# Turning the decayed keys for the state update on VectorE and through HBM instead of on TensorE, in a fused RWKV-6 and SiLU kernel

## The chip, the cores and the metric

The kernel runs on one core of a Trainium2 chip. The metric is the device time in microseconds of one execution. The profile is one execution of the same program, with 646.2 us from its first to its last instruction.

The engines are called by the names of the profile: PE is TensorE (PEld its weight loads), DVE is VectorE, ACT is ScalarE, POOL is GpSimd, SP is SyncE, which here issues transfers. An engine name with a q (SPq, ACTq) is the queue's own instructions, among them the issue of a transfer.

## The reference

Two blocks follow each other: a linear attention with a decay per channel, and a feed-forward block with SiLU.

```python
B, H, S, D = 4, 8, 768, 48
for t in range(S):
    kt, vt, rt, wt = k[:, :, t], v[:, :, t], r[:, :, t], w[:, :, t]
    cur = einsum('bhd,bhe->bhde', u * kt, vt)
    y[:, :, t] = einsum('bhd,bhde->bhe', rt, state + cur)
    state = wt[..., None] * state + einsum('bhd,bhe->bhde', kt, vt)
x = y.transpose(0, 2, 1, 3).reshape(3072, 384)     # tokens by model width
h = x @ w_in                                       # 384 by 2048
out = (h / (1 + exp(-h))) @ w_out                  # 2048 by 384
```

The change touches the last line of the loop only: the sum over the tokens of key times value that is added to the state.

## The kernel before

**Units.** The sequence is cut into 6 chunks of 128 tokens, and the 4 batches into 2 pairs. A unit is one chunk of one pair, so there are 12 units, numbered 0 to 11. A unit has 2 batches (index b) of 8 heads. Two heads are stacked on the partitions (64 rows each, of which 48 are channels), so that a batch has 4 tiles of 128 partitions by 128 tokens, numbered p; e is the head within the tile.

**Attention in a unit.** The recurrence inside a chunk is solved in 7 levels with doubling block sizes. `tk` holds the keys, channels on the partitions and tokens along the free dimension, in 16 rows of 128 tokens: 8 rows of "own" keys (batch and p), and two rooms of 4 rows each, X[0] and X[1], in which the odd blocks of a level are put together for the score matmuls. At each level POOL multiplies keys by decays (`grow_keys`, L491), DVE does so with the queries `tr`, and PE makes scores (`score_products`, L527). After level 6 the own keys hold, for each token, the key with the decay up to the end of the chunk. The second batch is kept with its tokens in reverse order.

**Then the unit's end.** `y_state` (L652) multiplies the old state by the queries, `y` (L665) adds score times value, ACT copies the sum to `yt` (L669), and `move_x` (L715) sends it by 10 transfers into `xt`, the input of the feed-forward block. `update` (L679) contracts keys and values over the tokens into `p_kv`; POOL decays the old state (L684), and DVE adds the two (L693). For this contraction the tokens have to lie on the partitions. In the units 2 to 11 `turn_k` does that: 4 transposes on PE for each batch (L639), 8 in a unit, and one copy on ACT from PSUM to `kq` for each batch (L640). In the last two units `update` returns at once, since no chunk follows; `turn_k` is run there all the same.

**The feed-forward block** of earlier units fills PE beside this. `up` (L757, 12 instructions of PE, 8 calls in a unit) writes `p_h`, which has two buffers and is emptied by SiLU on ACT (L763). `quarter` (L820, 7 calls in a unit) is a block product of the second weight by a scheme with 7 products instead of 8; its operands are made by `sums` on DVE (L802), and its result leaves through DVE (L829) and ACT (L827).

**What sets the order.** The program is written with a schedule by hand: each engine runs its instructions in the order in which they were emitted and stops at one whose wait is not met. Units 0 to 2 are written out step by step. For the units 3 to 11 `mix(i)` gives groups of steps of the attention, and after each group `ROOM` says how many steps of the feed-forward block follow. Before the change `turn_k` is a group of its own, with two calls of `up` ahead of it and one behind, then come `y_state`, `y`, `update` and `move_x`.

**Transfers.** Nearly all are issued by SP, in the order of emission. `load_blocks` (L106) fetches w, k and r of the unit after next in pieces of 32 tokens, 48 transfers in a unit. `load_values` (L119, L126), `load_rk` (L90) and the 4 small `diag` transfers (L425) are on the same queue, as are the results (L833). [...]

Of the kernel before, what the change touches and what calls it, by code (L numbers as in the profile page):

```python
# [8 lines left out]
F32 = mybir.dt.float32  # L9
# [29 lines left out]
def kernel(  # L39
# [11 lines left out]
    nc = tc.nc  # L51

    B, H, S, D = r.shape
    DM, DF = moe_w_in.shape
    L = 128
    NL = 7
    NB = 2
    NP = H // 2
    PD = 64
    Q = NB * NP  # L60
    NX = Q + 2 * NP
    X = 0, NP + Q
# [4 lines left out]
    NSLOT = 2  # L67
    NTOK = 2
# [28 lines left out]
    def load_blocks(i, name, g):  # L97


        n, b0 = units[i]  # L100
        src, t0 = {"w": w, "r": r, "k": k}[name], n * L + g * 32
        room = raw[:, i % NSLOT, WRK[name]].rearrange("p b h d -> p (b h d)").rearrange("p (q g d) -> p q g d", q=Q, d=32)
        for e in range(2):
            for a in range(2):
                d0, d1 = a * 32, min(D, a * 32 + 32)
                nc.sync.dma_start(out=room[(2 * e + a) * 32:(2 * e + a + 1) * 32, :, g, 0:d1 - d0],  # L106
                                  in_=src[b0:b0 + NB, e::2, t0:t0 + 32, d0:d1].rearrange("b q t d -> t (b q) d"))

    def load_values(i):
# [18 lines left out]
    def load_rk(i):  # L128

        for x, src in enumerate((r, k)):  # L130
            load_twos(tokens_rk[:, x].rearrange("p h s d -> p h (s d)"), src, i, [nc.sync] * NB)


    rounding = ExitStack()
    p_w = rounding.enter_context(tc.tile_pool(name="pr", bufs=1, space=bass.MemoryType.PSUM)).tile([128, 2, 512], F32, name="p_w")
# [188 lines left out]
    def turn(i, b, name):  # L324
        dst = {"w": tw, "r": tr, "k": tk}[name]
        if i not in dst:
            rows = NX if name == "k" else Q
            t = pt.tile([128, rows, L], F32, name="t" + name, bufs=2 if name == "r" else 1)
            dst[i] = [t] if name == "w" else t
        t = dst[i][0] if name == "w" else dst[i]  # L330
        if i < NTOK:
            if (i, b, name) not in turned:
                turn_in(i, b, name)
            turn_out(i, b, name, t)
        else:
            row0 = b * NP + (NP if name == "k" else 0)
# [17 lines left out]
    def turn_out(i, s, name, t):  # L354
        p_tr = turned.pop((i, s, name))
        if name == "k":
            to = t[:, NP:].rearrange("p q (i s) -> p q i s", s=2)
# [96 lines left out]
    def keys(i, start, *dims):  # L454
        k = tk[i][:]
        return bass.AP(tensor=k.tensor, offset=k.offset + start, ap=[k.ap[0], *dims])

    def odd_keys(i, l):

        c, blocks = 1 << l, NP * (L >> (l + 2))  # L460
        nc.scalar.copy(out=keys(i, X[(l + 1) % 2] * L + c, [4 * c, blocks], [c, 2], [1, c]),  # L461
                       in_=keys(i, NP * L + c, [4 * c, blocks], [NP * L + c, 2], [1, c]))

    def odd_products(i, l, b, *dims, skip=0):

# [10 lines left out]
    def grow_keys(i, l):  # L476
        c, ni = 1 << l, L >> (l + 1)
        x_at, next_at = X[l % 2], X[(l + 1) % 2]
        for b in range(NB):
            row0 = NP + b * NP  # L480
            if l + 1 < NL:
                start = [next_at * L, row0 * L][b] + b * c
                step = 2 * c + (1 - 2 * b) * (row0 - next_at) * L
                out = keys(i, start, [4 * c, NP * ni // 2], [step, 2], [1, c])
                have = keys(i, x_at * L + b * c, [4 * c, NP * ni // 2], [2 * c, 2], [1, c])
                blocks = [[4, NP * ni // 2], [2, 2]]
            else:
                out = keys(i, row0 * L + b * c, [L, NP], [1, c])
                have = keys(i, x_at * L + b * c, [L, NP], [1, c])
                blocks = [[2, NP]]  # L490
            nc.gpsimd.tensor_tensor(out=out, in0=have, in1=odd_products(i, l, b, *blocks), op=ALU.mult)  # L491
        if i < NTOK:
            product(i, l)

    def odd_ones(i):

        nc.scalar.copy(out=keys(i, X[1] * L + 1, [1, NB], [4, NP * L // 4], [1, 1]),
                       in_=keys(i, NP * L + 1, [NP * L + 1, NB], [4, NP * L // 4], [1, 1]))

    def start_keys(i, engine, own):  # L500

        n = NP * L // 4
        for b in range(NB):
            x = b if own else 1 - b
            at = (NP + b * NP) * L + b
# [116 lines left out]
    def turn_apart(i):  # L622

        apart[i] = [ps.tile([128, NB, NP, D], F32, name="p_sc", bufs=2) for e in range(2)]
        for x in range(Q):
            for e, to in enumerate(apart[i]):
                rows = slice(PD * e, PD * e + D)
                nc.tensor.transpose(to[:, x // NP, x % NP], tk[i][rows, NP + (x if x < NP else NP + Q - 1 - x), :],
                                    ident[rows, rows])

    def turn_k(i, b):
        kq[i, b] = pt.tile([128, NP, 2 * PD], F32, name="kq")
        if i < NTOK:
            for e, have in enumerate(apart[i]):
                nc.scalar.copy(out=kq[i, b][:, :, PD * e:PD * e + D], in_=have[:, b])
            return
        p_tr = ps.tile([128, NP, 2 * PD], F32, name="p_m", bufs=2)
        for p in range(NP):
            nc.tensor.transpose(p_tr[:, p, :], tk[i][:, NP + (p, 2 * NP - 1 - p)[b], :], ident)  # L639
        nc.scalar.copy(out=kq[i, b], in_=p_tr)  # L640

    p_yt, p_kv, yt = {}, {}, {}

# [27 lines left out]
    def update(i, b):  # L671
        n, b0 = units[i]
        if n == S // L - 1:
            return
        if b == 0:
            p_kv[i] = ps.tile([128, NB, NP, D], F32, name="p_m" if i < NTOK else "p_sc", bufs=2)
        for p in range(NP):
            for e in range(2):
                nc.tensor.matmul(p_kv[i][PD * e:PD * e + D, b, p, :], lhsT=kq[i, b][:, p, PD * e:PD * e + D],  # L679
                                 rhs=values(i, b)[:, 2 * p + e, :], start=(b == 0 and p == 0),  # L680
                                 stop=(b == NB - 1 and p == NP - 1))
        new = state[:, b0 + b]
        if n > 0:
            nc.gpsimd.tensor_tensor(out=new, in0=new,  # L684
                                    in1=tw[i][NL][:, b * NP:(b + 1) * NP, :].to_broadcast([128, NP, 2 * PD]),
                                    op=ALU.mult)
        if b < NB - 1:
            return
        for e in range(2):
            rows, cols = slice(PD * e, PD * e + D), slice(PD * e, PD * e + D)  # L690
            new = state[rows, b0:b0 + NB, :, cols]
            if n > 0:
                nc.vector.tensor_tensor(out=new, in0=p_kv[i][rows], in1=new, op=ALU.add)  # L693
            else:
                (nc.scalar.copy if i == 0 else nc.vector.tensor_copy)(out=new, in_=p_kv[i][rows])
# [23 lines left out]
    def both(fn, i, *args):  # L719
        return [(fn, i, b, *args) for b in range(NB)]  # L720
# [4 lines left out]
    def mix(i):  # L725
# [6 lines left out]
                  [(burst, i, 3), (keep_level, i, 3), (bonus_sum, i, 0), (bonus, i, 1), (bonus, i, 2)],  # L732
                  [(keep_level, i, 4), (go_on, i, 4)],
                  [(prepare, i, 5), (bonus_sum, i, 1)] + ([(load_rk, i + 1)] if i + 1 < len(units) else []),
                  [(burst, i, 5), (keep_level, i, 5)], [(keep_level, i, 6), (go_on, i, 6), (bonus_spread, i), (bonus_write, i)],
                  both(turn_k, i), [*both(y_state, i), *both(y, i), *both(update, i), (move_x, i)]]

        loads = block_loads(i + NSLOT) if i + NSLOT < len(units) else []
        if i + 1 < len(units):
# [164 lines left out]
    for m in range(6):  # L904
# [7 lines left out]
    do(blocks[2], (burst, 2, 3), (keep_level, 2, 3), (keep_level, 2, 4), (go_on, 2, 4), (prepare, 2, 5), (bonus, 2, 1),  # L912
       (bonus, 2, 2), (down, 0, 1, 2), (bonus_sum, 2, 1), (load_rk, 3), (sums, 1, 1), *blocks[3:7], (down, 0, 1, 3))
    do((burst, 2, 5), (keep_level, 2, 5), (keep_level, 2, 6), (go_on, 2, 6), (up, 1, 6), (bonus_spread, 2), (bonus_write, 2),
       (load_values, 3), *both(turn_k, 2), (weight_sums, 2), (up, 1, 7), (sums, 1, 2))
    do((sums, 1, 3), *both(y_state, 2), *both(y, 2), *both(update, 2), (move_x, 2),
       *blocks[7:])

    ROOM = 1, 1, 0, 2, 1, 1, 1, 1, 1, 2, 1, 2, 1, 0
    for i in range(3, len(units)):  # L920
        steps = downs(i - 2) + ups(i - 1)
        groups = mix(i)
# [40 lines left out]
```

## Time and profile before

| | us |
|---|---|
| time, median of 3 runs | 647.81 (647.59 to 648.37) |
| span of the profiled execution | 646.2 |
| PE busy, of the span | 639.6 (99%) |
| DVE busy | 433.9 (67%) |
| POOL busy | 283.1 (44%) |
| ACT busy | 203.8 (32%) |
| the 80 transposes of L639, sum of PE's busy time | 10.4 |
| the 20 copies of L640, sum of ACT's busy time | 10.7 |

Share of busy time alone doesn't say what bounds a kernel, so the profile also follows the chain of work that ended last, back from the last instruction: at each step to what released it. A row of that chain has the start, the length and the instructions it merges. A row of a group of instructions has the line, engine and operation, the tiles and shapes, the count, then the busy time, the mean in ns of one, and the idle time ahead of it with what ended that. A row of transfers has the count, the size and the median time from the issue to the landing. The transposes of this kernel have a pattern on PE that repeats from the third unit on with a period of 50.94 us (324.61 to 375.55 us for L639 in the chain).

### The profile page before, as it was taken

How to read it: one execution, taken by the hardware profiler on the slowest of the kernel's cores; microseconds unless marked ns; L12 is line 12 of the kernel's file. 1: busy time of each engine (PE TensorE's matmuls, PEld its weight loads, DVE VectorE, ACT ScalarE, POOL GpSimd, SP SyncE). 2: the span in 40 equal slices, each digit the busy share in tenths (PEclk: the TensorE clock that was granted, in tenths of full speed). 3: DMA queues.
4: the chain of work that ended last, by engine and by line, in shares of the span. 5: the costliest groups of instructions: out<-in, count | busy, mean ns of one | idle time of the engine just before them, and what ended most of it. 6: DMA issues, size and time to landing. Idle time of an engine off the chain costs nothing.

```text
span 646.2 us, 12889 instructions
## 1 busy us (share of the span) xinstructions
PE 639.6 (99%) x4878; PEld 579.2 (90%) x4878; DVE 433.9 (67%) x737; ACT 203.8 (32%) x408; POOL 283.1 (44%) x356
## 2 busy tenths in 40 slices
PE   8999999999999999999999999999999999999998
PEld 7888876898899899899899899899899989989997
DVE  7879789896777677586586586676586766751031
ACT  5798872212321321320321231231232232131120
POOL 6898398466065054254334425416416505510000
PEclk9999999999999999999999999999999999999999
DMA  9975954433534524513513513423432022000000
GB/s 229 276 180 131 229 129 50 91 75 52 96 63 69 96 49 72 88 31 64 98 29 67 96 28 58 96 37 52 90 54 38 26 50 50 27 2 25 25 0 25
DMA packets 201134, 49.21 MB, mean 76 GB/s; under 512 B 188912, under 2 KB 195952, under 8 KB 201072
## 3 DMA queue, kind: packets, MB, share of 16 engines
q1 hardware_dynamic: 199488, 47.79, 36.5%
q10 hardware_dynamic: 1584, 0.59, 0.4%
q8 instruction: 39, 0.64, 0.4%
q14 instruction: 23, 0.19, 0.1%
HBM read 39.52 MB, written 4.72 MB: 68 GB/s over the span
## 4 chain that ended last, share of the span: by engine, by line
PE 95%; DVE 2%; POOL 1%; ACT 1%; issue 1%; POOLq 0%; DVEq 0%; ACTq 0%
PE p_h L757 39%; PE p_o L820 31%; PE p_sc L527 6%; PE p_m L527 4%; PE p_m L776 3%; PE p_m L665 3%; PE p_m L652 3%; PE p_m L639 1%; PE p_sc L679 1%; POOL tk L491 1%; PE p_m L350 1%; PE p_m L855 1%; PE p_m L703 0%; DVE score L450 0%; POOL w_in_sb L227 0%
## 5 line engine op out<-in xcount | busy, mean ns | idle before, releaser
L757 PE MATMUL p_h<-xt,w_in_sb 128*128 128x256 f32 x1152 | 258.4, 382 | 0.7 <-POOL tk L507 0.7
L757 PEld LDWEIGHTS p_h<-xt,w_in_sb 128*128 128x128 f32 x1152 | 215.8, 190 | 32.5 <-POOL tk L507 0.9
L763 ACT ACTIVATE gt<-p_h 128x512 f32<-128x512 f32 x93 | 55.5, 596 | 228.2 <-PE p_h L757 228.1
L491 POOL TENSOR_TENSOR tk<-tk,tw 128x256 f32<-128x256 f32 x144 | 102.1, 732 | 23.3 <-ACT tk L461 16.6
L537 DVE COPY_PREDICATED score<-mask,p_sc 128x512 f32<-128x512 int8 x78 | 64.1, 885 | 59.7 <-PE p_sc L527 59.4
L820 PE MATMUL p_o<-own,temps 128*128 128x192 f32 x528 | 90.3, 328 | 0.4 <-DVE temps L829 0.4
L820 PE MATMUL p_o<-w_out_sb,gt 128*128 128x192 f32 x528 | 90.4, 328 | 0.0
L820 PEld LDWEIGHTS p_o<-own,temps 128*128 128x128 f32 x528 | 85.8, 190 | 1.8 <-DVE temps L829 0.7
L820 PEld LDWEIGHTS p_o<-w_out_sb,gt 128*128 128x128 f32 x528 | 85.9, 190 | 0.9 <-issue 0.4
L684 POOL TENSOR_TENSOR state<-state,tw 128x512 f32<-128x512 f32 x16 | 19.3, 1225 | 118.5 <-PE p_m L652 118.5
L386 POOL TENSOR_TENSOR tw<-tw 128x256 f32<-128x256 f32 (+6 forms) x83 | 39.8, 480 | 54.5 <-DVE tw L338 50.6
L802 DVE TENSOR_TENSOR temps<-gt 128x256 f32<-128x256 f32 x88 | 44.3, 504 | 21.9 <-ACT gt L763 21.9
L461 ACT COPY tk<-tk 128x256 f32<-128x256 f32 x60 | 24.6, 410 | 83.4 <-PE p_sc L527 40.8
L527 PEld LDWEIGHTS p_sc<-tr,tk 48*128 48x128 f32 x640 | 39.2, 186 | 12.1 <-issue 8.9
L473 DVE TENSOR_TENSOR tr<-tr,tw 128x512 f32<-128x512 f32 x53 | 46.0, 868 | 3.3 <-POOL tk L491 1.0
L527 PE MATMUL p_sc<-tr,tk 48*128 48x128 f32 x640 | 47.1, 285 | 0.6 <-POOL tk L491 0.6
L408 POOL TENSOR_TENSOR ruk<-tokens_rk 128x768 f32<-128x768 f32 x10 | 18.6, 1858 | 65.8 <-DVE own_sums L415 65.8
L595 DVE TENSOR_TENSOR tr<-tr,tw 128x512 f32<-128x512 f32 x29 | 39.9, 1375 | 1.3
L537 DVE COPY_PREDICATED score<-mask,p_m 128x512 f32<-128x512 int8 x54 | 35.4, 706 | 0.0
L820 PE MATMUL p_o<-w_out_sb,temps 128*128 128x192 f32 x176 | 30.4, 326 | 0.0
L829 DVE TENSOR_TENSOR partial<-p_o,partial 128x192 f32<-128x192 f32 x33 | 11.6, 353 | 27.6 <-PE p_o L820 27.6
L597 ACT COPY tr<-tr 128x512 f32<-128x512 f32 x29 | 18.4, 634 | 35.8 <-DVE tr L473 35.0
(144 smaller groups left out, 753.3 us busy)
## 6 DMA issues: line engine op xcount, KB each, us to landing
w_out_sb<-in_moe_w_in_dram SPq DMA_DIRECT2D x6, 768.0 KB, 6.9
tokens_rk<-in_r_dram SPq DMA_DIRECT2D x20, 192.0 KB, 3.4
tokens_rk<-in_k_dram SPq DMA_DIRECT2D x20, 192.0 KB, 3.8
w_out_sb<-in_moe_w_out_dram SPq DMA_DIRECT2D x4, 768.0 KB, 6.3
own<-in_moe_w_out_dram SPq DMA_DIRECT2D x4, 768.0 KB, 5.8
xt<-yt SPq DMA_DIRECT2D x60, 48.0 KB, 2.0
raw<-in_w_dram SPq DMA_DIRECT2D x80, 32.0 KB, 2.2
raw<-in_k_dram SPq DMA_DIRECT2D x80, 32.0 KB, 2.4
```

Source lines behind the costliest of these rows:

```text
L386: engine.tensor_tensor(out=up, in0=t[:, :, 0::2], in1=t[:, :, 1::2], op=ALU.mult)
L461: nc.scalar.copy(out=keys(i, X[(l + 1) % 2] * L + c, [4 * c, blocks], [c, 2], [1, c]), in_=keys(i, NP * L + c, [4 * c, blocks], [NP * L + ...
L473: nc.vector.tensor_tensor(out=odd, in0=odd, in1=tw[i][l][:, :, 0::2][:, :, :, None].to_broadcast([128, Q, L >> (l + 1), c]), op=ALU.mult)
L491: nc.gpsimd.tensor_tensor(out=out, in0=have, in1=odd_products(i, l, b, *blocks), op=ALU.mult)
L527: nc.tensor.matmul(bass.AP(tensor=s_p.tensor, offset=s_p.offset, ap=[s_p.ap[0], [apart * L // 2, 2], [1, L // 2]]), lhsT=tk[i][rows, X[l % ...
L537: nc.vector.copy_predicated(out=dst, mask=masks[l][:, :, None].to_broadcast([128, NB, NP, ni, c]), data=sc[e].rearrange("p (b q) (i c) -> ...
L595: nc.vector.tensor_tensor(out=new[:, :, :, 1, :], in0=old[:, :, :, 1, :], in1=tw[i][l][:, :, 0::2][:, :, :, None].to_broadcast([128, Q, L ...
L652: nc.tensor.matmul(p_yt[i, b][:, p, :], lhsT=state[:, b0 + b, p, :], rhs=tr[i][:, b * NP + p, :], start=(p == 0), stop=False)
L757: nc.tensor.matmul(p_h[:, a, :], lhsT=w_in_sb[:, c, f * 128:(f + 1) * 128], rhs=xt[i][:, c, :], start=(c == 0), stop=(c == KC - 1))
L763: nc.scalar.activation(out=gt[i, m], in_=p_h, func=AF.Silu)
L802: nc.vector.tensor_tensor(out=out, in0=one, in1=two, op=op)
L820: nc.tensor.matmul(p, lhsT=left(f), rhs=right[:, f, :], start=(f == 0), stop=(f == FH - 1))
```

## The change

From unit 2 on the keys are turned without PE. VectorE transposes each block of 32 by 32 in two instructions, from the own rows of `tk` into its first 8 rows, which are no longer needed after the last scores. A block then has its tokens and channels exchanged, but the blocks stand in the wrong places: the partition still says which 32 channels, and the free dimension which 32 tokens. Four transfers write the blocks to a scratch tensor in HBM in runs of 128 bytes, and four transfers read them back in runs of 512 bytes, so that they land at the right place in `kq`. The units 10 and 11 turn no keys at all. To make room for the transposed blocks, X[1] moves ahead of the own keys (rows 0 to 3, 4 to 7, and 8 to 15). `kq` is now one buffer for both batches. From unit 5's data on, the r part of `load_blocks` is issued by ACT instead of SP. The purpose is to free PE, PSUM and ACT from the turning.

```diff
-    X = 0, NP + Q
+    X = 0, NP
+    OWN = 2 * NP
...
-                nc.sync.dma_start(out=room[...], in_=src[...])
+                queue = nc.scalar if i > NTOK + NSLOT and name == "r" else nc.sync
+                queue.dma_start(out=room[...], in_=src[...])
...
+    scratch = ctx.enter_context(tc.tile_pool(name="scratch", bufs=2, space=bass.MemoryType.DRAM))
...
     def turn_k(i, b):
-        kq[i, b] = pt.tile([128, NP, 2 * PD], F32, name="kq")
-        if i < NTOK:
-            for e, have in enumerate(apart[i]):
-                nc.scalar.copy(out=kq[i, b][:, :, PD * e:PD * e + D], in_=have[:, b])
-            return
-        p_tr = ps.tile([128, NP, 2 * PD], F32, name="p_m", bufs=2)
-        for p in range(NP):
-            nc.tensor.transpose(p_tr[:, p, :], tk[i][:, NP + (p, 2 * NP - 1 - p)[b], :], ident)
-        nc.scalar.copy(out=kq[i, b], in_=p_tr)
+        if b == 0:
+            kq[i] = pt.tile([128, NB, NP, 2 * PD], F32, name="kq", bufs=1)
+        for e, have in enumerate(apart[i]):
+            nc.scalar.copy(out=kq[i][:, b, :, PD * e:PD * e + D], in_=have[:, b])
+
+    def turn_blocks(i):
+        for b in range(NB):
+            nc.vector.transpose(out=tk[i][:, b * NP:(b + 1) * NP, :], in_=tk[i][:, OWN + b * NP:OWN + (b + 1) * NP, :])
+        kept = scratch.tile([32, Q, 4, 4, 32], F32, name="kept_keys")
+        for x in range(4):
+            nc.sync.dma_start(out=kept[:, :, :, x].rearrange("t q g d -> t (q g) d"),
+                              in_=tk[i][x * 32:(x + 1) * 32, 0:Q].rearrange("t q (g d) -> t (q g) d", d=32))
+        kq[i] = pt.tile([128, NB, NP, 2 * PD], F32, name="kq", bufs=1)
+        for g in range(4):
+            nc.sync.dma_start(out=kq[i][g * 32:(g + 1) * 32].rearrange("t b q d -> t (b q) d"),
+                              in_=kept[:, :, g].rearrange("t q x d -> t q (x d)"))
...
+        back = b == 1 and i >= NTOK
-                nc.tensor.matmul(p_kv[i][...], lhsT=kq[i, b][:, p, PD * e:PD * e + D],
+                nc.tensor.matmul(p_kv[i][...], lhsT=kq[i][:, b, NP - 1 - p if back else p, PD * e:PD * e + D],
...
-                  [(burst, i, 5), (keep_level, i, 5)], [(keep_level, i, 6), (go_on, i, 6), (bonus_spread, i), (bonus_write, i)],
-                  both(turn_k, i), [*both(y_state, i), *both(y, i), *both(update, i), (move_x, i)]]
+                  [(burst, i, 5), (keep_level, i, 5)],
+                  [(keep_level, i, 6), (go_on, i, 6), (bonus_spread, i), *[(turn_blocks, i)] * (i < len(units) - NB), (bonus_write, i)],
+                  [*both(y_state, i), *both(y, i), *both(update, i), (move_x, i)]]
...
-       (load_values, 3), *both(turn_k, 2), (weight_sums, 2), (up, 1, 7), (sums, 1, 2))
+       (load_values, 3), (turn_blocks, 2), (weight_sums, 2), (up, 1, 7), (sums, 1, 2))
...
-    ROOM = 1, 1, 0, 2, 1, 1, 1, 1, 1, 2, 1, 2, 1, 0
+    ROOM = 1, 1, 0, 2, 1, 1, 1, 1, 1, 2, 1, 3, 0
```

`ROOM` loses the entry of the removed group and keeps its sum: three calls of `up` now stand between the turning and `y_state`.

More of the change, by code (lines that the diff above doesn't have):

```diff
@@ L105, in load_blocks @@
                 d0, d1 = a * 32, min(D, a * 32 + 32)
-                nc.sync.dma_start(out=room[(2 * e + a) * 32:(2 * e + a + 1) * 32, :, g, 0:d1 - d0],
+                queue = nc.scalar if i > NTOK + NSLOT and name == "r" else nc.sync
+                queue.dma_start(out=room[(2 * e + a) * 32:(2 * e + a + 1) * 32, :, g, 0:d1 - d0],
                                   in_=src[b0:b0 + NB, e::2, t0:t0 + 32, d0:d1].rearrange("b q t d -> t (b q) d"))
@@ L335, in turn @@
         else:
-            row0 = b * NP + (NP if name == "k" else 0)
+            row0 = b * NP + (OWN if name == "k" else 0)
             to, back = t[:, row0:row0 + NP, :], name == "k" and b == 1
@@ L356, in turn_out @@
         if name == "k":
-            to = t[:, NP:].rearrange("p q (i s) -> p q i s", s=2)
+            to = t[:, OWN:].rearrange("p q (i s) -> p q i s", s=2)
             nc.scalar.copy(out=to[:, 0:NP, :, s], in_=p_tr[:, :, 0])
@@ L461, in odd_keys @@
         nc.scalar.copy(out=keys(i, X[(l + 1) % 2] * L + c, [4 * c, blocks], [c, 2], [1, c]),
-                       in_=keys(i, NP * L + c, [4 * c, blocks], [NP * L + c, 2], [1, c]))
+                       in_=keys(i, OWN * L + c, [4 * c, blocks], [NP * L + c, 2], [1, c]))
     def odd_products(i, l, b, *dims, skip=0):
@@ L479, in grow_keys @@
         for b in range(NB):
-            row0 = NP + b * NP
+            row0 = OWN + b * NP
             if l + 1 < NL:
@@ L497, in odd_ones @@
         nc.scalar.copy(out=keys(i, X[1] * L + 1, [1, NB], [4, NP * L // 4], [1, 1]),
-                       in_=keys(i, NP * L + 1, [NP * L + 1, NB], [4, NP * L // 4], [1, 1]))
+                       in_=keys(i, OWN * L + 1, [NP * L + 1, NB], [4, NP * L // 4], [1, 1]))
     def start_keys(i, engine, own):
@@ L504, in start_keys @@
             x = b if own else 1 - b
-            at = (NP + b * NP) * L + b
+            at = (OWN + b * NP) * L + b
             have = keys(i, at + 2 * x, [4, n], [1, 1])
@@ L627, in turn_apart @@
                 rows = slice(PD * e, PD * e + D)
-                nc.tensor.transpose(to[:, x // NP, x % NP], tk[i][rows, NP + (x if x < NP else NP + Q - 1 - x), :],
+                nc.tensor.transpose(to[:, x // NP, x % NP], tk[i][rows, OWN + (x if x < NP else NP + Q - 1 - x), :],
                                     ident[rows, rows])
     def turn_k(i, b):
-        kq[i, b] = pt.tile([128, NP, 2 * PD], F32, name="kq")
-        if i < NTOK:
-            for e, have in enumerate(apart[i]):
-                nc.scalar.copy(out=kq[i, b][:, :, PD * e:PD * e + D], in_=have[:, b])
-            return
-        p_tr = ps.tile([128, NP, 2 * PD], F32, name="p_m", bufs=2)
-        for p in range(NP):
-            nc.tensor.transpose(p_tr[:, p, :], tk[i][:, NP + (p, 2 * NP - 1 - p)[b], :], ident)
-        nc.scalar.copy(out=kq[i, b], in_=p_tr)
+        if b == 0:
[13 more added lines that the diff above has]
+                              in_=kept[:, :, g].rearrange("t q x d -> t q (x d)"))
     p_yt, p_kv, yt = {}, {}, {}
@@ L676, in update @@
             p_kv[i] = ps.tile([128, NB, NP, D], F32, name="p_m" if i < NTOK else "p_sc", bufs=2)
+        back = b == 1 and i >= NTOK
         for p in range(NP):
             for e in range(2):
-                nc.tensor.matmul(p_kv[i][PD * e:PD * e + D, b, p, :], lhsT=kq[i, b][:, p, PD * e:PD * e + D],
+                nc.tensor.matmul(p_kv[i][PD * e:PD * e + D, b, p, :], lhsT=kq[i][:, b, NP - 1 - p if back else p, PD * e:PD * e + D],
                                  rhs=values(i, b)[:, 2 * p + e, :], start=(b == 0 and p == 0),
```

## The prediction

> **What bounds the kernel now.** I read the busy shares first, then the chain that ended last, then a unit of that chain in order of time.
>
> ```profile
> PE 639.6 (99%) x4878; PEld 579.2 (90%) x4878; DVE 433.9 (67%) x737; ACT 203.8 (32%) x408; POOL 283.1 (44%) x356
> PE 95%; DVE 2%; POOL 1%; ACT 1%; issue 1%; POOLq 0%; DVEq 0%; ACTq 0%
> ```
>
> PE is both the busiest engine and 95% of the chain. So what leaves PE is a gain, and whatever makes PE wait is a loss at full price. The chain from 324 us on shows the end of a middle unit (start, length, work):
>
> ```profile
> 324.61 0.87 PE p_m L639 x8
> 325.48 2.59 PE p_h L757 x12
> 328.07 1.78 PE p_m L652 x16
> 329.86 1.88 PE p_m L665 x32
> 331.74 0.72 PE p_sc L679 x32
> 332.46 10.60 PE p_o L820 x64
> ```
>
> The eight key transposes take 0.87 us of the chain. Between them and their reader, `update` (L679), lie 2.59 + 1.78 + 1.88 = 6.25 us of other work on PE. PE runs in order: if the keys aren't there when `update` is next, nothing behind it runs, though the quarters (L820) don't need them. The timeline of the same stretch gives ACT and SP:
>
> ```profile
> 321.25 2.50 DVE L450 COPY_PREDICATED score<-own_mask,both_b 128x1024 f32<-128x1024 int8 x2
> ...
> 331.79 0.58 ACT L669 COPY yt<-p_m 128x512 f32<-128x512 f32 x1 [0.29 <-PE p_m L665]
> ```
>
> The second copy to `yt` ends at 332.37, that is 0.63 us after PE's last `y` matmul (331.74). Unit 2 is different. There SP is the busy one:
>
> ```profile
> 122.57 2.10 SPq L106 DMA_DIRECT2D raw<-in_w_dram  x4
> 124.71 6.85 SPq L106 DMA_DIRECT2D raw<-in_k_dram  x12
> 131.66 0.40 SPq L782 DMA_DIRECT2D out_dram<-ob  x1
> 132.15 0.39 SPq L119 DMA_DIRECT2D vt<-in_v_dram  x1
> 132.64 2.15 SPq L126 DMA_DIRECT2D vq<-in_v_dram  x4
> 134.90 5.29 SPq L715 DMA_DIRECT2D xt<-yt  x8
> ```
>
> It issues one transfer after the other up to 134.8 us, while unit 2's `update` runs at 127.34 (chain of waits).
>
> [...]the trace has this instruction at 0.67 us for 128x512 (L338). [...]
>
> ```profile
> L855 PE MATMUL p_m<-ident x16: 421/421/476, 1.4 to 4.6; 128*128 128x128 f32 x16
> ```
>
> The same instruction takes 273 ns at 11.7 us; the first sixteen filled 3.68 us, sixteen later ones 1.97.
>
> **The change part by part.**
>
> *Removed from PE:* 8 transposes in each of the units 2 to 11, 10 x 0.87 = 8.7 us of the chain. This is the most that can be won. The 20 ACT copies of 0.59 us (L640) go too; ACT is 32% busy, so they give nothing.
>
> *Added on VectorE:* 2 x 0.67 = 1.3 us a unit ahead of the bonus write (L450), which ends at 323.75 before and about 325.1 then; `y` needs it at 329. Hidden. What VectorE does behind (the sums, instructions of 0.42 us) ends late by about that, but the wait below leaves room. The moved X[1] and the new row index cost nothing: same instructions, same shapes.
>
> *The trip through HBM, units 5 to 9.* The transposes end at about 322.6. If the eight transfers then ran freely, they would arrive near 332. But the waits in the changed kernel's instructions tell another story. [...] In the units 5 to 9 the fourth write to the scratch waits for the second of the 8 r loads that ACT issues at the unit's end. In ACT's order these stand behind the two copies to `yt`, and those wait for `y` on PE. So the last write can't go out before PE has finished `y`, exactly when PE wants the keys. From the end of `y`:
>
> - copy to `yt` ends: 0.63
> - second r load goes out one issue later (0.45, the median of L106): 1.08
> - it lands 2.2 later (median of the raw loads): 3.3
> - the fourth write goes out and lands. No row has 128-byte runs to HBM. Nearest are 1.9 us (results, 192 KB) and 3.8 (`tokens_rk`, 192 KB in 384-byte runs); I take the 2.9 of `vt`, 1024 runs of 192 bytes, as many runs as here: 6.2
> - the four reads wait for all writes; the last goes out three issues of 0.6 later (L715): 8.0
> - it lands 2.6 later (`vq`; bounds 2.0 from `xt` and 3.8): 10.6
>
> PE waits 10.6 us, by the bounds 8.0 to 13.2 (issues up to 0.65, raw landing 2.4). Queued behind `update` on PE are the quarters; behind the state's addition (L693) on VectorE the next unit's transposes (L338), and POOL waits for these. So the whole pattern shifts. Afterwards PE runs cold: like the start of the trace, about 1.7 us lost (bounds 0 and 2.5[...]); I take 1.8. Net: 10.6 + 1.8 - 0.87 = 11.5 a unit, five units: **+57.7**.
>
> *Units 3 and 4.* The same, but here the third r load holds up a write (unit 3: the fourth; unit 4: the third, with another behind it): 0.4 to 1.0 later. Net 12.2, twice: **+24.4**.
>
> *Unit 2.* No r load of ACT's is concerned, but the eight transfers stand behind the row of loads shown above. They start at 134.8 at the earliest; four writes, the last at 136.3, landed at 139.2; four reads out by 141.0, landed at 143.6. PE is at `update` at 127.34 - 0.87 = 126.5. Wait 17.1, net 17.1 + 1.8 - 0.87: **+18.0**, with bounds 13.5 to 22.
>
> *Units 10 and 11:* nothing turned, **-1.7**.
>
> *The r loads on ACT*, 16 issues in each of the units 3 to 9: 16 x 0.45 = 7.2 us of an engine that is idle two thirds of the time. Four stand ahead of a SiLU at 319.5 for which ACT idled 4.2 us; four delay the next SiLU from 322.05 to about 323.6, and PE needs that buffer of `p_h` at 324.4: hidden by 0.8. Eight run during PE's wait. Taking them off SP gives nothing, since SP spends most of the later units waiting.
>
> Sum: 57.7 + 24.4 + 18.0 - 1.7 = +98.4, so 647.8 + 98.4 = **746 us**. With all low bounds: 5 x 7.1 + 2 x 7.6 + 13.5 - 1.7 = +63 (711). With all high ones: 5 x 14.8 + 2 x 15.8 + 22 - 1.7 = +126 (774).
>
> **The rivals.**
>
> *All hidden.* The keys arrive within PE's 6.25 us, as for a transfer issued at once and landed in one trip. Then only the 8.7 us go: 639 us. For it speaks that SP mostly waits in the units 5 to 9; against it that two trips in sequence, 2 x 2.0 at the least plus seven issues, already fill the room, and unit 2's full queue.
>
> *The bare trip.* [...] The keys then arrive at 322.6 + 1.8 (issues) + 2.9 + 1.8 + 2.6 = 331.7, against 330.9 on PE: a wait of 0.8 a unit, which cancels the gain. Unit 2 remains at about +16.2, the units 10 and 11 give 1.7: 662 us. Against it: the r loads follow `y` in ACT's order whatever their speed.
>
> *Worse.* The r loads ahead of SiLU take longer than 0.65 us each, [...]so that PE also waits for `p_h`[...]. With 3 us more in each of eight units and every unit cold for 5 us: 746 + 24 + 6 = 776 us.
>
> **How the numbers follow.** Main case 0.83, bare trip 0.07, all hidden 0.04, worse 0.06. I predict 746. The range 708 to 772 holds the main case with nearly all of its bounds; it leaves out the two fast rivals and most of the slow one. Only "all hidden" is faster: 0.04; same 0.01; slower 0.95.
>
> **What would show it.** In the chain of waits of the changed kernel `update` would appear with a wait for transfers, eight times, about 10 us each and longest in unit 2. PE's share would fall to about 87%, its busy tenths dip once a unit up to unit 9, and the matmuls behind each dip take longer than their mean for some 3 us. The period of a middle unit would grow from 50.94 to about 62.5 us, and the last two units would keep their lengths less 0.87. The fourth write would go out about 3 us after the end of `y`. I am wrong if that write goes out before ACT's copies to `yt`; if the landings of the 128-byte writes lie far from 2.9 us; or if PE comes out of the wait at full speed, which takes some 14 us off.

## The result and the profile after

| | before | after |
|---|---|---|
| time, median us | 648.09 (647.59 to 648.48) | 766.27 (761.65 to 768.03) |
| ratio | 1 | 1.1813, 95% interval 1.1777 to 1.1848 |
| span of the profiled execution, us | 646.2 | 764.8 |

The kernel became 18% slower; 746 us was predicted, with a range of 708 to 772. The page of the kernel after gives PE's share, the granted PE clock in 40 slices, and the shares of the chain that ended last:

```profile
PE 656.9 (86%) x4798; PEld 594.0 (78%) x4798; DVE 442.3 (58%) x753; ACT 194.1 (25%) x388; POOL 285.5 (37%) x356
...
PEclk9899999679969979997997997999799699999999
...
PE 80%; DMA 8%; DVE 3%; POOL 3%; SPq 3%; issue 1%; ACT 1%; ACTq 1%; POOLq 0%; DVEq 0%
```

PE fell from 99% to 86% of the span, although it has 80 instructions less. Its busy time even rose, from 639.6 to 656.9 us, since some matmuls took longer: the granted clock dips once in each of the units 2 to 9 (to 0.50 in the unit shown further down), and its mean over the span is 0.922, against 1.000 before. Transfers, which had no part in the chain, now have 8% of it. PE's waits (us in all, times, longest) say which:

```profile
PE p_sc L692 <- DMA kq<-kept_keys: 95.6, 8, 17.3
PE p_sc L531 <- POOL tk L495: 4.5, 2, 3.9
PE p_h L531 <- POOL tk L495: 2.1, 1, 2.1
```

The first row is `update` (L679 before), eight times. The other two are score matmuls (L527 before) that hardly waited before; I had not foreseen them. The chain of a middle unit, which answers to the one shown of before, and after it SP's own waits at the writes to the scratch:

```profile
398.76 1.78 PE p_m L664 x16
400.55 1.91 PE p_m L677 x32
...
402.84 1.94 DMA raw<-in_r_dram
404.78 0.02 issue
404.80 2.79 DMA kept_keys<-tk
407.59 0.02 issue
407.60 0.58 SPq L651
...
409.53 3.21 DMA kq<-kept_keys
412.74 0.14 issue
412.88 1.52 PE p_sc L692 x32
414.40 11.79 PE p_o L834 x64
```

```profile
SPq L647 <- DMA raw<-in_r_dram: 46.5, 7, 7.3
```

Read it downwards: `y` (L677) ends at 402.45, only then a load of r goes out, when it has landed the last write to the scratch (L647) goes out, then four reads (L651), and at 412.88 `update` begins. In 7 units, 3 to 9, SP stood in front of a write until an r load had landed. And behind the wait `update` takes 1.52 us instead of 0.72, and the four quarters 11.79 instead of 10.60.

**Where the 118.6 us between the spans are.** Waits of `update`: 95.6. Slower matmuls just behind: 8 x 0.8 = 6.4 in `update`, and 14.6 in the eight stretches of quarters (11.47 to 12.89 us each, 99.4 in all, against 8 x 10.60): 21.0. Transposes gone: 10 x 0.87 = -8.7. That leaves 10.7, and one place has it: the first `up` behind the work of unit 1 (L771, L757 before), which stood at 96.48 us in the chain, stands at 107.26, before any key has been turned the new way. The timeline of before shows the score matmuls of level 1 of the units 0 and 1; that of after has the same two, and in the middle the ones of level 2 behind the first:

```profile
13.60 1.18 PE L527 MATMUL p_h<-tr,tk 48*128 48x128 f32 x16
39.22 1.18 PE L527 MATMUL p_sc<-tr,tk 48*128 48x128 f32 x16
```

```profile
16.12 1.18 PE L531 MATMUL p_h<-tr,tk 48*128 48x128 f32 x16 [2.10 <-POOL tk L495]
18.54 2.08 PE L531 MATMUL p_sc<-tr,tk 48*128 48x128 f32 x16
47.97 1.95 PE L531 MATMUL p_sc<-tr,tk 48*128 48x128 f32 x16 [3.87 <-POOL tk L495]
```

They now wait for `grow_keys` on POOL (L495), and the matmuls after the wait are slow (2.08 and 1.95 us where 1.16 to 1.18 is normal; the granted clock is 0.50 from 18 to 24 and from 49 to 51 us).

### The profile page after: what moved, and what is told of

Read it like the earlier page. It is cut to its first block, busy times and chain, and to the rows that moved or that the text cites. A ratio compares the mean times of both kernels' runs of the same rounds, so it can differ in the third digit from the quotient of the medians.

```text
span 764.8 us, 12748 instructions
## 1 busy us (share of the span) xinstructions
PE 656.9 (86%) x4798; PEld 594.0 (78%) x4798; DVE 442.3 (58%) x753; ACT 194.1 (25%) x388; POOL 285.5 (37%) x356
## 4 chain that ended last, share of the span: by engine, by line
PE 80%; DMA 8%; DVE 3%; POOL 3%; SPq 3%; issue 1%; ACT 1%; ACTq 1%; POOLq 0%; DVEq 0%
PE p_h L771 32%; PE p_o L834 29%; PE p_sc L531 5%; DMA kq<-kept_keys 3%; PE p_m L531 3%; PE p_m L677 2%; DMA kept_keys<-tk 2%; PE p_m L664 2%; PE p_m L790 2%; DMA raw<-in_r_dram 2%; SPq L651 2%; PE p_sc L692 2%; POOL tk L495 1%; PE p_m L354 1%; ACTq L108 1%
## 5 line engine op out<-in xcount | busy, mean ns | idle before, releaser
L771 PE MATMUL p_h<-xt,w_in_sb 128*128 128x256 f32 x1152 | 257.6, 382 | 0.7 <-POOL tk L511 0.7
L771 PEld LDWEIGHTS p_h<-xt,w_in_sb 128*128 128x128 f32 x1152 | 217.2, 190 | 33.3 <-POOL tk L511 0.9
L495 POOL TENSOR_TENSOR tk<-tk,tw 128x256 f32<-128x256 f32 x144 | 105.3, 754 | 34.0 <-ACT tk L465 23.6
L834 PE MATMUL p_o<-w_out_sb,gt 128*128 128x192 f32 x528 | 105.0, 363 | 0.0
L834 PEld LDWEIGHTS p_o<-w_out_sb,gt 128*128 128x128 f32 x528 | 100.5, 217 | 1.1 <-issue 0.4
L541 DVE COPY_PREDICATED score<-mask,p_sc 128x512 f32<-128x512 int8 x78 | 64.1, 885 | 59.7 <-PE p_sc L531 59.4
L834 PE MATMUL p_o<-own,temps 128*128 128x192 f32 x528 | 90.0, 328 | 0.0
L692 PE MATMUL p_sc<-vt,kq 128*48 128x48 f32 x128 | 7.1, 283 | 95.6 <-DMA kq<-kept_keys 95.6
L834 PEld LDWEIGHTS p_o<-own,temps 128*128 128x128 f32 x528 | 85.9, 190 | 1.1
L692 PEld LDWEIGHTS p_sc<-vt,kq 128*48 128x48 f32 x128 | 6.0, 190 | 97.4 <-issue 97.4
L706 DVE TENSOR_TENSOR state<-p_sc,state 48x384 f32<-48x384 f32 x16 | 8.9, 555 | 93.6 <-PE p_sc L692 93.5
L816 DVE TENSOR_TENSOR temps<-gt 128x256 f32<-128x256 f32 x88 | 43.5, 494 | 16.4 <-ACT gt L777 16.4
L841 ACT COPY partial<-p_o 128x192 f32<-128x192 f32 x11 | 3.5, 318 | 146.4 <-PE p_o L834 112.7
```

The costliest lines, as they stand in the source:

```text
L541: nc.vector.copy_predicated(out=dst, mask=masks[l][:, :, None].to_broadcast([128, NB, NP, ni, c]), data=sc[e].rearrange("p (b q) (i c) -> ...
L771: nc.tensor.matmul(p_h[:, a, :], lhsT=w_in_sb[:, c, f * 128:(f + 1) * 128], rhs=xt[i][:, c, :], start=(c == 0), stop=(c == KC - 1))
L816: nc.vector.tensor_tensor(out=out, in0=one, in1=two, op=op)
L834: nc.tensor.matmul(p, lhsT=left(f), rhs=right[:, f, :], start=(f == 0), stop=(f == FH - 1))
```

## The experiments

Each run was timed beside the kernel before (647.78 to 648.31 us there); the expectation of each was written ahead of it.

### What holds the keys: the place of r's loads

First, r's loads back on SP.

```diff
-                queue = nc.scalar if i > NTOK + NSLOT and name == "r" else nc.sync
+                queue = nc.sync
```

> The changed kernel with every load of r issued by SP again, the keys still turned through HBM. Theory (the fourth write waits for a load of r that stands behind ACT's copies to yt, so for the end of y): the four writes now wait only for loads issued long before. They go out when SP is free, at about 395.7 to 397.5 us in the unit that ends y at 402.45, land 2.8 later than the last issue, the reads take 1.8 of issue and 3.2 to land: keys at 405.2 to 407.2, so update waits 3 to 5 us instead of 10 in the units 3 to 9. Unit 2 stays at 17. Sum of the waits about 45 us instead of 95.6, time about 715 us (700 to 730). Rival (the round trip itself is too slow, whoever issues the loads): waits of 9 us and more stay, time above 750.

Measured: 704.89 us, ratio 1.0875 (1.0833 to 1.0916). The waits of `update` fell from 95.6 to 43.6 us, and SP's wait of 46.5 us for r at the writes is gone from its list.

```profile
PE p_sc L692 <- DMA kq<-kept_keys: 43.6, 8, 18.0
```

In the units 5 to 9 the waits of `update` are 1.6 to 3.6 us; unit 2 kept its 18.0, and unit 4 still had 10.2, where I had expected 3 to 5 in every unit from 3 on. So the round trip alone isn't what costs 10 us a unit. But this edit changes two things at once: the queue, and the place in ACT's order. The next one changes only the place.

```diff
-        behind = groups[3 if i > NTOK + 1 else 10:]
+        behind = groups[3 if i > NTOK + 1 else 10:-1]
```

> The changed kernel with r still issued by ACT, but no load put into the last group of a unit: all are emitted ahead of y, so in ACT's order none of them stands behind the copies to yt. Theory (what holds the fourth write is the place of r's loads behind the copies to yt, not that ACT issues them): in the units 5 to 9 update waits 1 to 4 us instead of 10; unit 2 stays at 17; units 3 and 4 open, since the loads crowd there. Time about 720 us (705 to 735). Rival (loads issued by ACT are late in themselves or slow the trip): about 10 us in every unit, above 750.

Measured: 714.39 us, ratio 1.1025 (1.1000 to 1.1051). SP's wait for r at the writes, and PE's wait at `update` in the units 2 to 9, in the timeline:

```profile
SPq L647 <- DMA raw<-in_r_dram: 0.2, 1, 0.2
```

```profile
156.94 0.88 PE L692 MATMUL p_sc<-vt,kq 128*48 128x48 f32 x16 [17.74 <-DMA kq<-kept_keys]
218.60 0.56 PE L692 MATMUL p_sc<-vt,kq 128*48 128x48 f32 x16 [1.40 <-DMA kq<-kept_keys]
273.49 0.88 PE L692 MATMUL p_sc<-vt,kq 128*48 128x48 f32 x16 [4.61 <-DMA kq<-kept_keys]
328.99 0.56 PE L692 MATMUL p_sc<-vt,kq 128*48 128x48 f32 x16 [2.94 <-DMA kq<-kept_keys]
384.25 0.88 PE L692 MATMUL p_sc<-vt,kq 128*48 128x48 f32 x16 [3.36 <-DMA kq<-kept_keys]
438.80 0.88 PE L692 MATMUL p_sc<-vt,kq 128*48 128x48 f32 x16 [2.73 <-DMA kq<-kept_keys]
493.70 0.88 PE L692 MATMUL p_sc<-vt,kq 128*48 128x48 f32 x16 [2.95 <-DMA kq<-kept_keys]
549.23 0.89 PE L692 MATMUL p_sc<-vt,kq 128*48 128x48 f32 x16 [3.83 <-DMA kq<-kept_keys]
```

With ACT still issuing r, the 10 to 11 us of the units 5 to 9 became 2.7 to 3.8. It is the place behind the copies to `yt` that held the write, not ACT as the issuer. What is left is the trip itself: in unit 6 the first write is issued at 374.05 us and the last read has landed at 384.12, 10.1 us later, while PE's `y` ends at 380.89, only 6.8 us after that first issue.

### The early loss: the rooms of tk

One part alone, put into the kernel before:

```diff
-    X = 0, NP + Q
+    X = 0, NP
+    OWN = 2 * NP
...
-        row0 = NP + b * NP
+        row0 = OWN + b * NP
```

> The kernel before with one part of the change alone: room X[1] in tk next to X[0], the own keys behind both. Keys turned on PE as before. Theory (the strided writes of grow_keys into X[0] and the own rows now span X[1], so in units 0 and 1 the score matmuls of an odd level wait for POOL's grow_keys of the same level): about 10.7 us lost, all of it before 110 us, time about 659 us. Rival (the early loss in the changed kernel comes from another of its parts, for instance kq with one buffer): 648 us, no difference.

Measured: 660.59 us, ratio 1.0188 (1.0173 to 1.0204), that is 12.3 us more than before, with PE's waits as in the kernel after:

```profile
PE p_sc L528 <- POOL tk L492: 5.0, 3, 3.9
PE p_h L528 <- POOL tk L492: 2.1, 1, 2.1
```

And the other way round, the kernel after with the old rooms:

```diff
-    X = 0, NP
-    OWN = 2 * NP
+    X = 0, NP + Q
+    OWN = NP
```

> The changed kernel with the rooms of tk where they were before (X[0], own keys, X[1]); the second block transpose then writes over own keys that the first has already read. Theory: the 10.7 us of the units 0 and 1 come back, the waits of update stay at about 95 us: 755 to 756 us. Rival (the early loss is not from the rooms): 766 us.

Measured: 754.90 us, ratio 1.1640 (1.1621 to 1.1659). That is 11.4 us less than after; PE's waits for `tk` in the scores shrink to 0.6 us, those for the keys stay (96.0). Both directions agree: moving X[1] next to X[0] costs 11 to 12 us, nearly all of it in the units 0 and 1. Up to the first `up` behind unit 1 (96.48 us before, 107.26 after) the kernel after has PE idle for 9.0 us instead of 3.0, and busy for 98.3 instead of 93.4, so about half of the loss is the wait and half the slow matmuls behind it. The size isn't fixed. In the profiles of the six kernels that turn keys through HBM and have X[1] moved (the kernel after and five of the experiments), `y` of unit 2 ends 7.9 to 14.3 us later than in the one of this experiment, although up to there they differ in nothing that an edit touches; PE's waits for `tk` differ by hardly more than 1 us. So differences of a few us between these kernels needn't come from their edits. Why the wait is there is not shown; I read it from the code only: `grow_keys` writes the next room and the own rows with one strided instruction, and X[1], which PE reads in the odd levels, now lies between the two. It was not tried with the instruction split.

### The slow matmuls: PE's clock

Work that nobody uses, put into the wait:

```diff
-                  [*both(y_state, i), *both(y, i), *both(update, i), (move_x, i)]]
+                  [*both(y_state, i), *both(y, i), *[(beat, 64)] * (i < len(units) - NB), *both(update, i), (move_x, i)]]
```

> The changed kernel with 64 transposes of the identity on PE between y and update in the units 2 to 9 (their result is used by nobody), about 7.9 us of PE work at full clock inside each wait of 10 us. Theory (the slow matmuls behind each wait are PE's clock after an idle stretch): the keys come no earlier, update starts at the same distance from the end of y, but update and the quarters behind it run at full speed again: the 21 us of excess (0.8 in update, 1.8 in the quarters, eight times) mostly go, time about 745 to 750 us. Rival (they are slow for another reason, such as transfers that land at the time): update still takes 1.5 us and the quarters 12.5, time 766 us.

Measured: 770.28 us, ratio 1.1886 (1.1862 to 1.1910). A miss: nothing was won. (Of the 4.7 us by which its profile is longer than that of the kernel after, 3.4 lie ahead of the end of `y` in unit 2, before the first of these waits.) The 64 transposes took 7.2 us, the keys came later than they ended, and PE was idle for 3.2 to 10.8 us all the same. Behind such a gap `update` again took 1.3 to 1.5 us. That said either that 3.2 us of idle time are enough, or that the clock is not the cause. The same with 88 transposes (140 in unit 2):

> As the kernel with 64 transposes of the identity ahead of update, but with 88 of them (9.9 us at 113 ns each; 140, so 15.8 us, in unit 2), so that less than 1 us of the wait is left idle. With 64, 3.9 us were left idle and update and the quarters were as slow as without. Theory (PE's clock falls in an idle stretch, and 3.9 us already is one): update takes 0.9 us or less, the quarters 10.6; about 18 to 21 us less than the changed kernel, 746 to 750 us. Rival (slow for another reason, such as the transfers that land there): update 1.5 and quarters 12.5 as before, 766 us or a little more.

Measured: 753.69 us, ratio 1.1626 (1.1609 to 1.1644). The chain of this kernel, two of the eight units:

```profile
281.59 1.52 PE p_sc L692 x32
283.12 12.90 PE p_o L834 x64
...
406.19 0.93 PE p_sc L692 x32
407.11 10.60 PE p_o L834 x64
```

In the first the gap left was 4.0 us, in the second 0.7. In five of the eight units (gaps of 0.7 to 2.5 us) the quarters took 10.60 again; in the other three (2.3 to 4.0 us) 11.6 to 12.9. The time fell by 12.6 us against the kernel after. In the profiles `update` and the quarters of the eight units are 13.3 us shorter, the keys come 3.4 us later in sum, and unit 2's `y` ends 3.0 us earlier. The clock that the profile shows as granted says the same directly. Here are stretches of the kernel after (the wait, `update` with the first quarters, the work behind) and, last, one of this kernel behind the gap of 0.7 us; the number after the last bracket is the clock as a share of full speed:

```profile
402.50:406.40 3.90, 0.00 (x0) 0.00 (x0) 1.34 (x4) 0.56 (x1) 0.00 (x0) 1.00 0.35 43
412.90:416.70 3.80, 3.80 (x39) 3.71 (x40) 2.17 (x4) 0.00 (x0) 0.00 (x0) 0.50 0.17 43
418.00:426.00 8.00, 8.00 (x51) 7.90 (x49) 3.68 (x7) 2.11 (x4) 6.89 (x13) 1.00 0.33 43
...
406.20:417.70 11.50, 11.50 (x98) 11.22 (x98) 7.58 (x12) 2.13 (x4) 7.08 (x12) 1.00 0.30 52
```

So the clock is the cause. Most of what missed the expected 746 to 750 is in the three units whose gap I had not closed: 6.0 us in their `update` and quarters.

### Hiding the wait, and what then waits

`update` isn't needed until two units later. It can stand in the next unit.

```diff
-                  [*both(y_state, i), *both(y, i), *both(update, i), (move_x, i)]]
+                  [*both(y_state, i), *both(y, i), (move_x, i)]]
...
+    AT = 4
...
+            if at == AT:
+                do(*both(update, i - 1))
```

> The changed kernel with update of a unit moved behind the second burst of scores' start of the next unit (after the keep of level 1), so that two calls of quarter at least and one burst (over 10 us of PE) stand between y and update. The trip through HBM is as slow as ever. Theory (the loss is nothing but PE standing in front of an update whose keys come 10 us late, with the cold clock that follows): the waits of 95.6 us and the 21 us of slow matmuls go, 648 to 653 us, with the loss in the units 0 and 1 still in it. Rival (the transfers or VectorE's work hold up something else too, as values, xt or the next unit's loads): well above 660.

> As the kernel with the late update, with the rooms of tk where they were before the change as well. Theory: the early loss goes too, and what is left is the gain that the change was after: 648.1 less ten times 0.87, so 638 to 641 us. Rival (the trip costs something else): 648 or more.

Measured: 695.77 us, ratio 1.0725 (1.0707 to 1.0743), and with the old rooms 680.59 us, ratio 1.0511 (1.0464 to 1.0558; its profile is of an execution of 685.94 us). Both missed by some 40 us. PE's waits for the keys are gone, as expected; but in the waits of the second there are new ones, on PE and on VectorE, and the timeline shows one of them:

```profile
PE p_o L834 <- DVE temps L843: 16.4, 7, 8.3
PE p_h L771 <- ACT gt L777: 5.9, 1, 5.9
PE p_sc L692 <- DVE score L541: 5.0, 8, 1.5
...
DVE tk L342 <- DMA kept_keys<-tk: 33.3, 5, 8.4
```

```profile
424.33 1.31 DVE L342 STREAM_TRANSPOSE tk<-raw 128x512 f32<-128x512 f32 x2 [4.71 <-DMA kept_keys<-tk]
```

`tk` has one buffer, and the last write to the scratch reads it. While that write is held, VectorE can't put the next unit's keys into `tk`, and what stands behind in its order, with the additions of the quarters' results (L843), comes late for PE. A second wait had been standing right behind the first. A second buffer for `tk`, the direct test, was not tried. So the held write had to go as well, with r's loads ahead of `y`:

> The kernel with the late update and the rooms of before, with r's loads emitted ahead of y as well. With the late update alone VectorE stood in front of the next unit's key transposes into tk (five waits for the writes to scratch, 33.3 us together), because tk has one buffer and the fourth write reads it until about 6 us after y; the sums of the quarters stand behind. Theory (a second wait behind the first: the held write keeps tk as well as the keys): from unit 4 on the fourth write now lands by about the end of y, VectorE's waits for kept_keys shrink to unit 2's 8 us and little more, and 10 to 16 us go: 664 to 671 us; what stays above 640 is mostly unit 2, where SP's full queue still sets the write. Rival (VectorE is late for another reason, such as the added transposes or the update's new place): 676 us or more.

Measured: 680.03 us, ratio 1.0507 (1.0490 to 1.0523). The step was right and the time wrong. VectorE's wait for the writes fell from 33.3 us to unit 2's 7.3, PE's wait for VectorE at the quarters (L834) from 16.4 to 7.2. But PE's waits for VectorE and ACT together hardly fell: 31.8 us before (the three rows of PE above, and 4.5 for ACT at the quarters), 30.6 now. Two rows that grew show why:

```profile
ACT gt L777 <- DMA raw<-in_r_dram: 33.0, 9, 7.6
...
PE p_h L771 <- ACT gt L777: 18.5, 7, 8.8
```

The loads of r, now ahead of SiLU in ACT's order, wait themselves or take ACT's time to be issued (the profile doesn't part the two), and SiLU stands behind them with the buffer of `p_h` that PE wants. The next kernel changes three more places: in unit 2 the turning is emitted ahead of the loads, `update` stands after two quarters, and POOL's decay keeps its old place.

```diff
-       (load_values, 3), (turn_blocks, 2), (weight_sums, 2), (up, 1, 7), (sums, 1, 2))
+       (turn_blocks, 2), (load_values, 3), (weight_sums, 2), (up, 1, 7), (sums, 1, 2))
...
+            if at == 2:
+                do(*both(update, i - 1))
```

> As the kernel before it, with three edits more: in unit 2 the turning is emitted ahead of 16 loads of unit 4 and of the loads of v, so that SP issues the writes at once; update stands after two quarters of the next unit, ahead of the burst, so that it needn't wait for p_sc; the decay of the state on POOL stays where it was. If the whole loss of the change is in what waits for the trip (PE for the keys, VectorE for tk) plus the rooms, this kernel keeps only the gain: 638 to 645 us, faster than before. Rival (PE waits somewhere else as soon as these are gone, since SP has 8 transfers more in each unit and VectorE 1.3 us): 648 to 660 us.

Measured: 666.39 us, ratio 1.0295 (1.0280 to 1.0309). Above the expectation, and above the rival's 648 to 660 as well, with the rest in three units: PE waits for the keys 10.0 us in the units 2 to 4 and 7.4 us for SiLU in the units 3 and 4, where the loads are crowded. From unit 5 on PE doesn't wait at all, and the chain shows what the change can bring at best:

```profile
348.88 1.78 PE p_m L664 x16
350.67 1.89 PE p_m L677 x32
352.55 5.40 PE p_o L841 x32
357.95 0.85 PE p_sc L702 x32
358.81 5.40 PE p_o L841 x32
...
399.29 1.78 PE p_m L664 x16
```

The period is 50.41 us against 50.94. Of the 0.87 us of transposes, 0.13 go back to `update` (0.85 for 0.72) and 0.20 to the quarters, now in two stretches (10.80 for 10.60). To take only that gain, the next kernel turns keys on PE up to unit 4 and through HBM from unit 5 on:

> The rooms of before; the keys of the units 2 to 4 turned on PE as before, where SP's queue is full; in the units 5 to 9 blocks through HBM, with update after two quarters of the next unit and r's loads (from unit 7's data on) issued by ACT ahead of y; nothing turned in the units 10 and 11. In the kernel before this one the units 5 to 9 ran without a wait of PE at a period of 50.41 us against 50.94 before. Theory (the gain of the change is there once nothing waits for the trip): 648.1 less 5 times 0.53 less 2 times 0.87, so 643.7 (643 to 645.5). Rival (the clean units were clean only because earlier waits had given SP and VectorE time): 648 or more.

Measured: 648.13 us beside 647.94 for the kernel before, ratio 1.0007 (0.9999 to 1.0016): no difference, against an expected 643.7. The later units kept their 50.40 us. But unit 5, where the new order begins, has the crowded loads now: in PE's timeline it waits 2.3 us for SiLU, which stood 3.5 us behind loads of r, and 1.6 us for the keys.

```profile
275.50 2.86 PE L787 MATMUL p_h<-xt,w_in_sb 128*128 128x256 f32 x12 [2.33 <-ACT gt L793]
...
289.03 0.56 PE L709 MATMUL p_sc<-vt,kq 128*48 128x48 f32 x16 [1.61 <-DMA kq<-kept_keys]
```

From the `y_state` of unit 4 to that of unit 6 that kernel takes 2.9 us more than the one before. The later units give four times 0.54 and once 0.88, 3.0 in all, and so it is eaten up.

### The one part that pays

```diff
-                  both(turn_k, i), [*both(y_state, i), *both(y, i), *both(update, i), (move_x, i)]]
+                  both(turn_k, i) if i < len(units) - NB else [], [*both(y_state, i), *both(y, i), *both(update, i), (move_x, i)]]
```

> The kernel before with one part of the change alone: no keys turned in the units 10 and 11, where nothing reads them. Theory: 16 transposes leave PE, the bound engine, 2 times 0.87 = 1.7 us, so 646.3 (646.0 to 646.6). Rival (the copies on ACT or the PSUM buffers they held mattered too): 645 or less; rival (PE waits there for something else anyway): 648.

Measured: 646.34 us against 647.94, ratio 0.9976 (0.9967 to 0.9984). In its chain the period up to unit 9 is 50.94 as before, and the two that hold the dropped transposes are 50.06 and 49.35 us, against 50.94 and 50.23: 0.88 each. The gain is small, 0.24%, but its interval is clear of 1. It is the only part of the change that gained anything where it was tried alone; r's loads on ACT and the one buffer of `kq` were not tried alone.

## Why the prediction was right, and where its sum was off

The direction, the size (746 for 766) and the main mechanism held. By its own steps:

- **PE bounds, and a wait is paid in full: right.** The waits of 95.6 us are all in the span: in the unit shown `update` starts at 412.88 us and the quarters, which don't need the keys, only behind it at 414.40.
- **The fourth write waits for an r load behind `y`: right, and shown.** SP's 46.5 us at the writes are gone when r is issued by SP, and fall to 0.2 when only the place in ACT's order changes; with that PE's 10 to 11 us of wait become about 3. What ties the write to that load the traces don't show; they show only that it goes out when the load has landed. The signs that were named came too: the write goes out 2.4 us after the end of `y`, and the period of a middle unit is 62.5 to 64.1 us.
- **The length of the trip: right in sum, not in each term.** In the unit shown, from the end of `y`: r goes out after 0.4 us (1.1 predicted), is in at 2.3 (3.3), the write in at 5.1 (6.2), the last read out at 7.1 (8.0), in at 10.3 (10.6). The first term was too long, since ACT's issue of the load starts beside the second copy to `yt` (both at 402.48 in the timeline) and not after it. The last was too short (3.2 for 2.6). That the two cancel is luck. So it is in unit 2: SP reached the writes 6.9 us after the end of `y` instead of 8.3, and the trip took 10.3 us instead of 8.8. Over the units 5 to 9 the waits were 10.2 to 11.0; units 3 and 4: 11.5 and 13.3 for about 11.3; unit 2: 17.3 for 17.1. Sum 95.6 for 92.7. The low bound of 8.0 us in the prediction doesn't follow from its own terms, which give 9.0 with the shortest landings.
- **The cold clock: right in kind, too small.** That PE comes out of a wait slower was assumed: the profile of before has no wait that shows it, and its granted clock is 1.000 in the mean. The kernel after shows it, with 0.50 behind the wait. The term, 1.8 us a unit, was an estimate from the start of the trace. It measured 2.6: 0.8 in `update`, which I had left out as a victim, and 1.8 in the quarters. This is 6.6 us of the miss.
- **"The moved X[1] and the new row index cost nothing: same instructions, same shapes": wrong.** This is the step that failed. The instructions are the same, but what they wait for isn't. It cost 10.7 us in this profile (12.3 and 11.4 in the two runs on it alone), half of the difference between 746 and 766. No bound of the prediction held it: 766 lies within 708 to 772 only because the width that was given to other terms happened to be free for it. The view that would have told it was there: which instruction writes between which rows, and who reads the rows between.
- **VectorE's two added transposes and the r issues on ACT cost nothing: right for this kernel, in which PE was waiting.** Its waits have no row of PE for SiLU, so the rival "worse" didn't come true in that point. In the kernels in which r's loads were also moved ahead of `y`, they held PE up through SiLU (18.5 us in one kernel, 2.3 in another). What VectorE's two transposes cost by themselves was not measured.
- **Units 10 and 11, -1.7: right**, 1.6 measured in the part alone.
- **The rival "bare trip" (662 us)**, in which nothing holds the writes up, put the trip at 9.1 us from the end of the turning and the wait at 0.8 a unit. Where the writes were no longer held, the units 5 to 9 waited 1.6 to 3.8 us, with the clock's loss behind most of them; so it was too cheap.
- **The rival "all hidden" (639 us)** was not reached by any arrangement that was tried. The best the middle units showed is 0.5 us each.

As sums: waits +2.9, cold +6.6, rooms +10.7. Together 20.2, which is 766.3 - 746.2 = 20.1 within the rounding and the difference between profile and median.

## What to carry to other kernels

Ask of a transfer not only how long it takes but what it waits for before it goes out: here the last write stood until a load on another queue had landed (46.5 us in 7 units), and that load stood, in its queue's order, behind copies that waited for the very engine that wanted the data. Before moving work off a bound engine, compare what leaves it (here 0.87 us a unit) with how short the cover is in which the replacement must arrive (here less than 7 us for a trip of 10 through HBM). And when a wait is moved away, look at who else was covered by it; here VectorE came up first and then, once loads had been moved ahead of SiLU, ACT; and the simplest part, not doing work that nobody reads, was all that was left of the gain: 1.6 us.

## What the runs showed of the hardware

In the kernel after the granted clock fell from 1.00 to 0.50 about 2.5 us into the wait of unit 2 and about 4.1 us into that of unit 6 (an estimate, worked out from its mean of 0.89 over 137.9 to 141.0 us and of 0.76 over 405.0 to 408.0, and from 0.50 as the lower clock). The waits for the keys in this kernel and the experiments show no sharp limit. Behind gaps of 0.7 to 1.9 us, and once of 2.5, the matmuls of `update` ran at full speed (0.93 us for both batches). Yet once, after 1.90, the quarters behind were slow (12.28 us for 10.60), although `update` had taken 0.92. Behind 2.30 us `update` took 1.42 and behind 2.73 already 1.52, while behind 3.22 us, in which PE waited for SiLU in one of the later kernels, the 12 matmuls of `up` took 2.86 us, as they did behind 0.55 (behind 4.15 us they took 4.45). Behind every wait for the keys of 3.36 us and more in these profiles `update` took 1.5 us. A wait of 17 us cost no more than one of 4 (1.52 us in `update` and 12.69 in the quarters behind the first, 1.52 and 12.90 behind the second). And transposes of the identity in the wait kept the matmuls behind it fast: where 88 of them had taken 9.8 us and the gap left was under 1 us, `update` took 0.93 us and the quarters 10.60, and the granted clock of the stretch shown, from 406.20 us on, was 1.00.

Loads that ACT issues delayed ACT's own work, although that work doesn't read them: in the kernel with the late `update` and r's loads ahead of `y`, SiLU stood 33.0 us in sum and up to 7.6 us at a time behind loads of r that ACT had to issue first.
